# An mLSTM cell with a multiplicative FFN: where the rest products stand, what fills step 2, and how the denominator is computed

## The chip, the cores and the metric

The kernel runs on one core of one Trainium2 chip. The core has five instruction streams that run side by side and wait for one another through semaphores: PE (TensorE, matrix products; PEld is its weight loading), DVE (VectorE), ACT (ScalarE), POOL (GpSimd) and SP (SyncE, which issues most DMA transfers). The metric is the time on the device in microseconds (us), the median over runs of the same kernel. A profile is one execution, taken down instruction by instruction.

## The reference

The first part is an mLSTM cell with batch 4, 8 heads, 768 time steps and head dimension 40. For every head it carries a matrix state C, a vector n and a running maximum m:

```python
m_new = max(f + m, i);  f_stab = exp(f + m - m_new);  i_stab = exp(i - m_new)
C = f_stab * C + i_stab * outer(v, k);   n = f_stab * n + i_stab * k
denom = max(abs(n . q), 1.0)
y = sigmoid(o) * (C @ q) / denom
```

The outputs y of 8 heads side by side make rows of 320 numbers, 3072 of them (4 x 768). The second part is a feed-forward network on these rows x, with 1024 hidden columns:

```python
out = ((x @ w1) * (x @ w2)) @ w3 @ w_out
```

All arrays that the kernel reads and writes hold float32 numbers, except that the four weight matrices come as 64-bit words, which the kernel has to turn into float32 itself.

## The kernel before, in words

**The cell.** The recurrence is computed in chunks of 64 time steps. Two chunks (128 rows, one per partition) of one batch with all 8 heads are a unit; there are 24 units n, n = 4c + b for the pair of chunks c (0 to 5) and the batch b. The main loop runs over steps s = 0 to 31 (L820). `quarter_work(s)` (L338) treats two units in one step: the outputs of unit s - 1 and the scores of unit s.

For the outputs TensorE computes `ph` (weights `pw` times values `v`, L363) and `pi` (queries times the carried state, L366). Both lie in the bank pair `cell[1]` of the products' memory: `pi` in columns 0 to 164, `ph` in columns 164 to 328. For the scores it computes `ss` (keys times queries, L389) and `pc` (values times keys, the state's update, L394) in `cell[0]`. In the traces `ph` and `pi` from unit 2 on are called `cell<-v_all,pw` and `cell<-state,qT`, and `ss` and `pc` `cell<-qT,kT` and `cell<-vw,kbuf`.

VectorE follows with `outputs()` (L419): `h` is `pi` scaled by a gate (L423) with `ph` added in four pieces (L430). Each value tile has a 41st column that is filled with ones, so column 40 of `h` is n . q, the number whose absolute value goes into the denominator. The generator `steps()` hands out the denominator's passes one at a time, so that they can be put between others: the absolute value (L438, 8 numbers per row), max with 1 and times 2 (L440), the reciprocal (L441) together with e = (tanh(o/2) + 1) x that (L443, 320 numbers per row), and y = h x e (L445, 320 numbers). The gate o was turned into tanh(o/2) on ScalarE (L270). Between these passes stand `first_read` (L397, which multiplies the scores by the weights) and the two additions to the state (L404 or L406, and L414). The units' y is brought to the FFN's layout: for units 0 to 14 by transposes on TensorE (`px`, L485) and a copy on ScalarE (`xT`, L486), for the later ones by way of DRAM.

**The FFN.** `w3 @ w_out` is computed once, in 8 pieces `wp` (L263) into `w3o`, as the weights arrive: ScalarE and VectorE turn each weight tile into float32 (`scale`, `convert`; VectorE's lines L199 and L200, and L248 which transposes w3). The products x @ w1 and x @ w2 (`pa` and `pb`) need 320 rows of the weights: two full slices of 128 (`up`, L628) and a rest of 64. The rest of both matrices stands in one tile `wr`, and the products with it are of 64x64 tiles of TensorE's array, four of which can work beside each other. They are made by `up_rest` (L634; 16 products a block, then ScalarE's copy L638 and VectorE's product L639) in steps 2 to 15, and by `left` inside `up_by_seven` (L721; 32 products, then four additions on VectorE, by the helper's lines L686 and L684) from step 19 on. `up_by_seven` makes the full slices of the later token groups with seven products for eight. `ffn_out` makes the down-projection `po` and ScalarE copies it out as `o_sb` (L741), and sends it off (L743). From step 19 to step 24 the down-projection lies in `cell[1]`, columns 0 to 320 (L871).

**How a step is put together.** The list `n_up` gives one block of `up` in each of the steps 2 to 5 and two in each of the steps 6 to 15; `n_seven` gives one `up_by_seven` to each of the steps 19 to 30; `n_down` gives two down-projections to the steps 16 to 20 and one to 21 to 24. In a step TensorE first does the folding `wp`, the full slices and the down-projections; then `quarter_work` is called, which calls `rest()` (L883: `up_rest` of the step's blocks, or `left`), then `ph` and `pi`, then `ss` and `pc`. Step 2 is special: between its outputs and its scores it calls `between()` (L892), which makes the first transposes of y, converts weights, and does its own block of `up`.

**What sets the order.** `in_order` (L84) ties every matrix product to the one before it, so TensorE works in the order of the program's text. The other engines keep the program's order too, up to the places marked with `issue_after`, which let instructions be put behind a given one. A pool of four rotating banks (`mps`, L77) holds all products other than the cell's; a product that takes a bank has to wait until the reader of that bank's last content is done. Where `cell` is used, the wait is for that pair's last reader.

`warm(n, m, small)` (L97) makes products that nobody reads: n of 128x512 and `small` ones of 64x64 with 64 columns. `between()` calls `warm(1, small=38)` between the transposes of units 0 and 1. `rows_of_u(n)` (L293) is one VectorE transpose of 128x512 (L295) that prepares the weights of unit n.

Of the kernel before, what the change touches and what calls it, by code (L numbers as in the profile page):

```python
# [16 lines left out]
def kernel(  # L17
# [26 lines left out]
    nc = tc.nc  # L44
# [46 lines left out]
    def mm(out, lhsT, rhs, start=True, stop=True):  # L91
        in_order(nc.tensor.matmul(out, lhsT=lhsT, rhs=rhs, start=start, stop=stop))  # L92
# [1 line left out]
    def transpose(out, in_, n=P):  # L94
        in_order(nc.tensor.transpose(out, in_, ident[0:n, 0:n]))  # L95

    def warm(n, m=4, small=0):  # L97
        bank = mps([P, 4, P], "fill")
        for _ in range(n):
            mm(bank[:, 0:m], ident, ident.unsqueeze(1).to_broadcast([P, m, P]))  # L100
        for i in range(small):
            r = halves[i % 2]
            mm(bank[r, 0, 0:L], ident[r, 0:L], ident[r, 0:L])

    halves = [slice(0, L), slice(L, P)]
    heads = [slice(0, D), slice(DP, DP + D)]
# [231 lines left out]
    def quarter_work(s, rest, between, late):  # L338


        rest()

        def part(j, c0, n):
            return cell[j][:, :, c0:c0 + NP * n].rearrange("p x (n d) -> p x n d", d=n)

# [21 lines left out]
        den = None  # L367
        if 0 <= s - 1 < NU:
            den = outputs(s - 1, pi, ph)
            den()  # L370
            if between:
                for _ in range(3):
                    den()
                den = None
                between()
            if late:
                late()
# [41 lines left out]
    def outputs(n, pi, ph):  # L419
        c, b = divmod(n, B)  # L420
        hs = slice(b * H, (b + 1) * H)
        h = sb.tile([P, H, D1], FP, name="h", tag="h")
        nc.vector.tensor_tensor(out=h.rearrange("p (n two) d -> p two n d", two=2), in0=pi,  # L423
                                in1=gT[:, c, hs].rearrange("p (n two) -> p two n", two=2).unsqueeze(3)
                                .to_broadcast([P, 2, NP, D1]), op=OP.mult)
        if n < N_DIAG:
            nc.vector.tensor_tensor(out=h, in0=ph, in1=h, op=OP.add)
        for x, e in quarters if n >= N_DIAG else ():
            part = h[halves[x], 0:H // 2] if x == e else h[halves[x], H // 2:H]
            nc.vector.tensor_tensor(out=part, in0=ph[x][halves[e]], in1=part, op=OP.add)  # L430

        den = sb.tile([P, H, 1], FP, name="den", tag="den")

        def steps():
            V = nc.vector
            yield V.tensor_scalar(out=den.bitcast(U32), in0=h[:, :, D:D1].bitcast(U32), scalar1=0x7FFFFFFF, scalar2=None,  # L438
                            op0=OP.bitwise_and)
            yield V.tensor_scalar(out=den, in0=den, scalar1=1.0, scalar2=2.0, op0=OP.max, op1=OP.mult)  # L440
            yield V.reciprocal(out=den, in_=den)  # L441
            e = o_t.pop(n)
            nc.vector.scalar_tensor_tensor(out=e, in0=e, scalar=1.0, in1=den.to_broadcast([P, H, D]), op0=OP.add, op1=OP.mult)  # L443
            y_t[n] = sb.tile([P, DM + REM], FP, name="y", tag="y")
            yield nc.vector.tensor_tensor(out=y_t[n][:, 0:DM].rearrange("p (h d) -> p h d", d=D), in0=h[:, :, 0:D],  # L445
                                           in1=e, op=OP.mult)

        done = steps()
        return lambda: next(done)

# [80 lines left out]
        if i < NBQ:  # L531
            nc.gpsimd.memset(qbuf[i][:, :, D:DP], 0.0)
    for i in range(NBV):
        nc.gpsimd.memset(vbuf[i][:, :, D:D1], 1.0)
    for t in state:
        nc.gpsimd.memset(t[0], 0.0)
    nc.gpsimd.memset(gates[:, 5 * TC:2 * TB], 0.0)
# [282 lines left out]
    for s in range(len(n_up)):  # L820
# [71 lines left out]
        def between():  # L892
            twice(1)
            weighted(2)
            rows_of_u(3)
            for _ in range(3):
                scale_next()
            for n in range(2):
                x_trans(n)
                if n == 0:  # L900
                    warm(1, small=38)
            for _ in range(3):
                convert()
            turn(2)
            block = up(*now[0])
            weighted(3)
# [105 lines left out]
```

## Time and profile before

| what | value |
|---|---|
| time, median of 3 runs | 426.51 us (425.51 to 427.06) |
| span of the profiled execution (first to last instruction) | 425.8 us, .7 under the median; the profile gives no other time of its own |
| mean granted clock of TensorE | 0.996 |
| TensorE busy | 414.1 us, 97% |
| VectorE busy | 313.5 us, 74% |
| ScalarE, GpSimd busy | 150.1 and 154.3 us, 35% and 36% |
| L438, L440, L441 (denominator, 8 numbers): median of 24 | .17, .16, .19 us |
| L443, L445 (320 numbers): median of 24 | .76 and .82 us (.49 to 1.44) |
| DMA | 51.15 MB, 120 GB/s on the mean |

A line of a timeline holds the start in us, the duration, the engine, the line of the program, the operation, what it writes and reads, the shape, and how many such instructions the line sums up (x16). In brackets stand the idle time of the engine just ahead and what ended it: `[0.58 <-DVE ab L639]` is .58 us of waiting for VectorE's instruction of line 639 that writes `ab`. "issue" is a wait for which the profile shows no other instruction. The products of one group overlap, so the next group's start says more than a duration added to a start.

### The profile page before, as it was taken

How to read it: one execution, taken by the hardware profiler on the slowest of the kernel's cores; microseconds unless marked ns; L12 is line 12 of the kernel's file. 1: busy time of each engine (PE TensorE's matmuls, PEld its weight loads, DVE VectorE, ACT ScalarE, POOL GpSimd, SP SyncE). 2: the span in 40 equal slices, each digit the busy share in tenths (PEclk: the TensorE clock that was granted, in tenths of full speed). 3: DMA queues.
4: the chain of work that ended last, by engine and by line, in shares of the span. 5: the costliest groups of instructions: out<-in, count | busy, mean ns of one | idle time of the engine just before them, and what ended most of it. 6: DMA issues, size and time to landing. Idle time of an engine off the chain costs nothing.

```text
span 425.8 us, 13079 instructions
## 1 busy us (share of the span) xinstructions
PE 414.1 (97%) x5353; PEld 335.3 (79%) x5353; DVE 313.5 (74%) x635; ACT 150.1 (35%) x404; POOL 154.3 (36%) x211
## 2 busy tenths in 40 slices
PE   7989989999999999999999999999999999999996
PEld 4768878888688788787777778788778879888896
DVE  6676986888949779778736966596868699575971
ACT  4766865567723623630433313032311110210000
POOL 4421342233303303303307751546453587542100
PEclk9989999999999999999999999999999999999999
DMA  8999998598977776985425675756421120000001
GB/s 186 204 173 245 214 144 140 134 193 180 215 183 154 166 182 135 181 164 105 89 80 130 153 141 121 142 133 117 87 44 36 35 39 2 31 2 31 2 32 62
DMA packets 135211, 51.15 MB, mean 120 GB/s; under 512 B 109360, under 2 KB 126960, under 8 KB 135152
## 3 DMA queue, kind: packets, MB, share of 16 engines
q1 hardware_dynamic: 131552, 46.29, 53.9%
q10 hardware_dynamic: 3600, 4.03, 2.7%
q8 instruction: 42, 0.69, 0.7%
q14 instruction: 17, 0.14, 0.1%
HBM read 44.50 MB, written 5.80 MB: 118 GB/s over the span
## 4 chain that ended last, share of the span: by engine, by line
PE 53%; issue 20%; DVE 7%; POOL 7%; SPq 7%; DMA 5%; ACT 1%; POOLq 0%; DVEq 0%
PE cell L92 17%; PE pa L92 12%; PE o L92 8%; PE pb L92 8%; PE p L92 3%; POOL pw L308 3%; SPq L184 3%; DVE w3T L666 2%; PE pt L95 1%; POOL vw L330 1%; SPq L148 1%; DMA raw<-in_moe_w_dram 1%; PE fill L92 1%; POOL raw L659 1%; POOL state L335 1%
## 5 line engine op out<-in xcount | busy, mean ns | idle before, releaser
L335 POOL TENSOR_TENSOR state<-state,decay 128x164 f32<-128x164 f32 x40 | 20.0, 500 | 154.8 <-DVE state L404 129.0
L92 PE MATMUL pa<-xT,w 128*128 128x256 f32 x240 | 60.4, 382 | 0.0
L92 PEld LDWEIGHTS pa<-xT,w 128*128 128x128 f32 x240 | 44.4, 190 | 6.8 <-DVE h L430 0.4
L303 ACT ACTIVATE pw<-pw,aT 128x64 f32<-128x64 f32 x184 | 46.4, 339 | 3.2 <-ACT o_sb L741 1.9
L92 PE MATMUL pb<-xT,w 128*128 128x256 f32 x192 | 45.4, 379 | 0.0
L729 POOL TENSOR_TENSOR ab<-ab,a_sb 128x512 f32<-128x512 f32 x22 | 29.4, 1356 | 32.2 <-DVE ab L684 32.2
L92 PEld LDWEIGHTS pb<-xT,w 128*128 128x128 f32 x192 | 36.4, 190 | 5.0
L711 POOL TENSOR_TENSOR wo<-wo 128x512 f32<-128x512 f32 x22 | 27.4, 1268 | 29.8 <-DVE wo L686 29.8
L92 PE MATMUL pa<-xT,wr 64*64 64x256 f32 x384 | 37.0, 386 | 0.5 <-DVE wr L200 0.5
L92 PE MATMUL wp<-wo,w3T 128*128 128x320 f32 x128 | 35.9, 433 | 1.1 <-DVE ab L639 0.6
L308 POOL TENSOR_SCALAR_AFFINE_SELECT pw<-pw 64x512 f32<-64x512 f32 x48 | 35.8, 746 | 3.0 <-ACT pw L303 1.2
L92 PE MATMUL pb<-xT,wr 64*64 64x256 f32 x384 | 36.4, 380 | 0.0
L92 PE MATMUL cell<-w3o,ab 128*128 128x320 f32 x128 | 35.4, 432 | 0.0
L638 ACT ACTIVATE a_sb<-pa 128x512 f32<-128x512 f32 x24 | 14.3, 598 | 59.0 <-PE pb L92 59.0
L639 DVE TENSOR_TENSOR ab<-pb,a_sb 128x512 f32<-128x512 f32 x24 | 16.4, 688 | 23.2 <-ACT a_sb L638 22.8
L92 PEld LDWEIGHTS wp<-wo,w3T 128*128 128x128 f32 x128 | 23.8, 190 | 10.5 <-DVE ab L639 0.8
L92 PEld LDWEIGHTS cell<-w3o,ab 128*128 128x128 f32 x128 | 24.3, 190 | 9.5
L92 PEld LDWEIGHTS pa<-xT,wr 64*64 64x64 f32 x384 | 18.9, 132 | 15.4 <-issue 8.8
L686 DVE SCALAR_TENSOR_TENSOR a_sb<-pa,wo 128x512 f32<-128x512 f32 x12 | 8.3, 689 | 29.8 <-PE pa L92 29.8
L430 DVE TENSOR_TENSOR h<-cell,h 64x164 f32<-64x164 f32 x88 | 28.6, 326 | 1.6
L92 PE MATMUL po<-w3o,ab 128*128 128x320 f32 x96 | 26.4, 433 | 0.0
L92 PEld LDWEIGHTS po<-w3o,ab 128*128 128x128 f32 x96 | 18.1, 190 | 7.3
(180 smaller groups left out, 846.4 us busy)
## 6 DMA issues: line engine op xcount, KB each, us to landing
raw<-in_moe_w_dram SPq DMA_DIRECT2D x64, 128.0 KB, 3.4
kbuf<-in_k_dram SPq DMA_DIRECT2D x24, 160.0 KB, 4.5
v_all<-in_v_dram SPq DMA_DIRECT2D x24, 160.0 KB, 4.9
o_in<-in_o_gate_dram SPq DMA_DIRECT2D x24, 160.0 KB, 4.8
pw<-U_d SPq DMA_DIRECT2D x28, 128.0 KB, 3.5
raw<-in_moe_w_dram SPq DMA_DIRECT2D x5, 512.0 KB, 6.7
raw<-in_moe_w_out_dram SPq DMA_DIRECT2D x8, 320.0 KB, 4.1
gates<-in_k_dram SPq DMA_DIRECT2D x28, 80.0 KB, 2.5
```

What stands on the lines that cost most here:

```text
L92: in_order(nc.tensor.matmul(out, lhsT=lhsT, rhs=rhs, start=start, stop=stop))
L184: nc.sync.dma_start(out=dst, in_=src)
L303: nc.scalar.activation(out=pw[:, h, :], in_=src[:, h, :], func=AF.Exp, bias=aT[:, c, b * H + h:b * H + h + 1])
L308: nc.gpsimd.affine_select(out=pw[r], in_=pw[r], compare_op=OP.is_ge, fill=0.0, base=0, pattern=[[0, H], [1, L]], channel_multiplier=-1)
L335: nc.gpsimd.tensor_tensor(out=new, in0=old, op=OP.mult, in1=decay[:, b * NP:(b + 1) * NP, 2 * c + x:2 * c + x + 1] .to_broadcast([P, NP, D1]))
L430: nc.vector.tensor_tensor(out=part, in0=ph[x][halves[e]], in1=part, op=OP.add)
L638: nc.scalar.mul(out=a_sb, in_=pa, mul=UP ** -2)
L639: nc.vector.tensor_tensor(out=ab_t[gr][j][:, fs[0]:fs[-1] + 1, t0:t0 + a_sb.shape[-1]], in0=pb, in1=a_sb, op=OP.mult)
L666: nc.vector.tensor_tensor(out=dst, in0=p, in1=q, op=OP.subtract)
L686: nc.vector.scalar_tensor_tensor(out=out, in0=p, scalar=UP ** -2, in1=q, op0=OP.mult, op1=OP.add)
L711: aside_by.tensor_tensor(out=kept[j][:, 1:4:2], in0=kept[j][:, 1:3], in1=kept[j][:, 3:4].to_broadcast([128, 2, TH]), op=OP.add)
L729: aside_by.tensor_tensor(out=t[:, f:FO:FH, :], in0=t[:, f:FO:FH, :], in1=a, op=OP.mult)
```

## The change

There are four edits.

1. `rest()` is no longer called first in `quarter_work`, but after the products `ph` and `pi` and VectorE's `h`. TensorE's order in a step becomes: full slices, down-projection, `ph`, `pi`, rest products, `ss`, `pc`. On VectorE `h` (L423, L430) stands ahead of L639, or of the four additions of `left`; the denominator's passes follow these.
2. In `between()`, `warm(1, small=38)` becomes `warm(2)`: the 38 small products go and one more of 128x512 is made.
3. In `between()`, `rows_of_u(3)` stands behind the three `convert()`.
4. The denominator takes four passes for five. The values' 41st column holds 2 in place of 1, so column 40 of `h` is 2r with r = n . q. The passes are: the reciprocal 1/(2r); its absolute value (8 numbers each); v = min(that, .5) x h (320 numbers); y = (tanh(o/2) + 1) x v (320 numbers). Since .5 / max(|r|, 1) = min(1/(2|r|), .5), y is the same. In the program's order the pass that makes v stands where the reciprocal's step ended, ahead of the second state addition (L414).

```diff
-    def warm(n, m=4, small=0):
+    def warm(n, m=4):
         bank = mps([P, 4, P], "fill")
         for _ in range(n):
             mm(bank[:, 0:m], ident, ident.unsqueeze(1).to_broadcast([P, m, P]))
-        for i in range(small):
-            r = halves[i % 2]
-            mm(bank[r, 0, 0:L], ident[r, 0:L], ident[r, 0:L])
...
     def quarter_work(s, rest, between, late):
-        rest()
...
             den = outputs(s - 1, pi, ph)
+        rest()
+        if den:
             den()
...
-            yield V.tensor_scalar(out=den.bitcast(U32), in0=h[:, :, D:D1].bitcast(U32), scalar1=0x7FFFFFFF, scalar2=None,
-                            op0=OP.bitwise_and)
-            yield V.tensor_scalar(out=den, in0=den, scalar1=1.0, scalar2=2.0, op0=OP.max, op1=OP.mult)
-            yield V.reciprocal(out=den, in_=den)
-            e = o_t.pop(n)
-            nc.vector.scalar_tensor_tensor(out=e, in0=e, scalar=1.0, in1=den.to_broadcast([P, H, D]), op0=OP.add, op1=OP.mult)
+            yield V.reciprocal(out=den, in_=h[:, :, D:D1])
+            yield V.scalar_tensor_tensor(out=den, in0=den, scalar=-1.0, in1=den, op0=OP.mult, op1=OP.max)
+            v = h[:, :, 0:D]
+            yield V.scalar_tensor_tensor(out=v, in0=den.to_broadcast([P, H, D]), scalar=0.5, in1=v, op0=OP.min, op1=OP.mult)
             y_t[n] = sb.tile([P, DM + REM], FP, name="y", tag="y")
-            yield nc.vector.tensor_tensor(out=y_t[n][:, 0:DM].rearrange("p (h d) -> p h d", d=D), in0=h[:, :, 0:D],
-                                           in1=e, op=OP.mult)
+            yield V.scalar_tensor_tensor(out=y_t[n][:, 0:DM].rearrange("p (h d) -> p h d", d=D), in0=o_t.pop(n), scalar=1.0, in1=v,
+                                         op0=OP.add, op1=OP.mult)
...
-        nc.gpsimd.memset(vbuf[i][:, :, D:D1], 1.0)
+        nc.gpsimd.memset(vbuf[i][:, :, D:D1], 2.0)
...
         def between():
             twice(1)
             weighted(2)
-            rows_of_u(3)
             for _ in range(3):
                 scale_next()
             for n in range(2):
                 x_trans(n)
                 if n == 0:
-                    warm(1, small=38)
+                    warm(2)
             for _ in range(3):
                 convert()
+            rows_of_u(3)
             turn(2)
```

Two consequences follow. The line numbers of the changed kernel are 3 to 5 smaller from `warm` on. And since the state's columns are made from the same value tiles, the state's 41st column is doubled as well.

## The prediction

> **What bounds the kernel now.** I read the page first: its busy line, and the clock row beside it (PEclk is 9, full, in all slices but the third, an 8).
>
> ```profile
> PE 414.1 (97%) x5353; PEld 335.3 (79%) x5353; DVE 313.5 (74%) x635; ACT 150.1 (35%) x404; POOL 154.3 (36%) x211
> ```
>
> TensorE is busy for 414.1 of the span's 425.8 us at a full clock, so 11.7 us in all can be saved by waiting less; anything that makes TensorE wait anew lengthens the kernel one for one. An engine off TensorE's path can lose time for nothing. The chain of waits says the same (PE 53%, DVE 7%, ACT 1%), so from here I read only the timelines of TensorE and, around the moved instructions, those of its partners.
>
> The outputs' products `ph` lie in the bank pair `cell[1]`, columns 164 to 328; from step 19 on the down-projection uses columns 0 to 320 of the same pair, and ScalarE has to copy it out (L741) before `ph` may write. TensorE's timeline of step 19, then ScalarE's for the same stretch:
>
> ```profile
> 256.62 0.70 PE L92 MATMUL cell<-w3o,ab 128*128 128x320 f32 x2
> 257.25 1.10 PE L92 MATMUL pa<-xT,wr 64*64 64x256 f32 x16
> 258.17 1.04 PE L92 MATMUL pb<-xT,wr 64*64 64x256 f32 x16
> 259.03 0.63 PE L92 MATMUL cell<-v_all,pw 64*64 64x41 f32 x32
> ```
>
> ```profile
> 257.36 0.43 ACT L741 COPY o_sb<-cell 128x320 f32<-128x320 f32 x1 [9.27 <-PE cell L92]
> 257.82 0.34 ACTq L743 DMA_DIRECT2D out_dram<-o_sb  x1
> 258.20 0.43 ACT L741 COPY o_sb<-cell 128x320 f32<-128x320 f32 x1 [0.41 <-ACT o_sb L741]
> ```
>
> Both copies start after the whole burst of down-projections and end at 258.63; the 32 rest products cover that, so `ph` at 259.03 waits for nothing.
>
> The second place is where VectorE converts w3 ahead of steps 8 and 9's adds; its timeline behind step 9's products, then TensorE's:
>
> ```profile
> 106.59 1.13 DVE L248 STREAM_TRANSPOSE w3T<-w 128x512 f32<-128x512 f32 x1
> 107.65 1.24 DVE L639 TENSOR_TENSOR ab<-pb,a_sb 128x512 f32<-128x512 f32 x2
> 108.81 0.48 DVE L423 TENSOR_TENSOR h<-cell,gT 128x328 f32<-128x328 f32 x1
> 109.33 1.34 DVE L430 TENSOR_TENSOR h<-cell,h 64x164 f32<-64x164 f32 x4
> ```
>
> ```profile
> 107.22 0.55 PE L95 MATMUL px<-ident,y 128*128 128x128 f32 x3
> 108.35 8.88 PE L92 MATMUL wp<-wo,w3T 128*128 128x320 f32 x32 [0.58 <-DVE ab L639]
> ```
>
> `wp` takes a bank that the first L639 frees: TensorE already waits 0.58 us for it here. The third is step 2, with the tiny products that go:
>
> ```profile
> 22.96 0.83 PE L95 MATMUL px<-ident,y 128*128 128x128 f32 x3 [1.19 <-DVE y L445]
> 23.59 4.90 PE L92 MATMUL fill<-ident 128*128 128x512 f32 x78
> 28.41 0.55 PE L95 MATMUL px<-ident,y 128*128 128x128 f32 x3
> ```
>
> **Part 1, rest() behind ph and pi, steps 19 to 24: +5.2 us.** Nothing now lies between the down-projection and `ph`, so each of these steps waits for the copies. From the rows: end of the last copy less the start of the next product, 258.62 - 257.25 = 1.37 and 277.07 - 275.70 = 1.37 with two copies, and .53 in each of the four steps with one (289.84 to 290.37, 303.97 to 304.50, 318.10 to 318.63, 332.23 to 332.77). Together 4.9, and .05 each for the release (px starts .05 after y's end at 22.91): 5.2. Bounds 4.9 to 5.6 (.12 each). The rest products take as long as before, behind the wait instead of in it. Queued behind the waiting `ph` on TensorE: pi, rest, ss, pc, the whole step; who waits for these in turn is part 2.
>
> **Part 2, the adds of the rest products come later on VectorE: +1.7.** VectorE now does h (.49 + 1.34) before the adds L686/L684. Counted from ph's start: h starts at +1.21 (in step 16, without rest products, `ph` starts at 218.20 and h at 219.41), ends at +3.09, the first add ends at +3.7, the others .6 apart, the fourth at +5.5. The next step's first `pa` takes the bank that the first add frees, and TensorE comes to it at +3.60 (260.85 - 259.03 for ph to pc, and 1.78 of rest products): +.15 with the release in each of steps 19 to 23, .75. In step 25 the product `p` takes such a bank. On the old times, step 24's `ph` would start at 332.23 + .58 = 332.8; TensorE comes to `p` after ph, pi (1.02) and the rest (1.78) at 335.7, the add ends at 332.8 + 3.7 = 336.5, and with the release it is +.95. Bounds .5 (only the last, and half of it) to 2.2 (.25 in the five). In steps 6, 7 and 10 to 15 the first add L639 ends at +3.7 to +3.8 and the next `pt` or `wp` wants it at +4.0: nothing, .27 to spare. Steps 16 to 18 have no rest.
>
> **Part 3, the same in steps 8 and 9: +2.05.** VectorE's conversions hold it to 107.72. Then h (.48 + 1.34, 1.85 with the starts) now goes ahead of L639, which is what `wp` waits for: 108.35 becomes 110.2, +1.85. One step earlier the conversions end at 92.94, .6 after pi: +.2. Bounds 1.2 (the conversions start earlier by the .63 us that VectorE is idle ahead of them at 100.28) to 2.6 (a bank of the second L639, .6 later, is wanted as well).
>
> **Part 4, the tiny products, and U's rows: -0.8.** 28.41 - 23.59 = 4.8 us of products go, one 128x512 (.59 at full clock) comes. But px of y(1) needs y(1), which ends at 25.62; the new passes bring it to about 25.0 and the idle time of 1.19 before 22.96 down by some .8. `pa` of step 2 (29.67) could start near 26.7, since the xT copies stand behind ScalarE's scalings to 25.8: 3 us. Those 3 us meet the weights. ScalarE's timeline of steps 3 and 4:
>
> ```profile
> 42.48 0.69 ACT L191 ACTIVATE raw<-raw 128x512 f32<-128x512 f32 x1 [1.20 <-DMA raw<-in_moe_w_dram]
> ...
> 44.48 0.69 ACT L191 ACTIVATE raw<-raw 128x512 f32<-128x512 f32 x1 [0.74 <-DMA raw<-in_moe_w_dram]
> ```
>
> These tiles land when the DMA queue brings them (97% busy from 30 to 61 us), not when TensorE is early. `pb` of step 4 needs the first through VectorE (45.16 before, not ahead of 44.5), wr the second (47.27; TensorE waits .51 there, and that gap goes, since ph and pi now stand ahead of it). But L639 of step 4 stands behind h and ends near 51.2, so `pa` of step 5 starts where it did, 51.3. In step 5 the same reckoning gives `pa` of step 6 at 59.0 against 60.59, if TensorE's 1.49 us without instructions (57.57 to 59.05, cause "issue") falls into a wait. I take half, .8. Bounds -3.3 (the 3 us stay, and half of U's row, .70, which no longer stands ahead of three conversions) and +1.0 (nothing gained, and half clock, which the row below shows, for 2 us more while TensorE idles ahead of px). That every row counts, 8.0, is rival 3. rows_of_u(3) after the conversions delays weights(3) on ScalarE and masks(3) on POOL by 3.9 us (25.54 to 29.46) at the most; their first reader is L397 of step 3 at 45.08, and ph of step 4 at 48.24 the first on TensorE.
>
> **Part 5, order of tile shapes: +0.5.** From ph's start to pi's is .49 behind 128x128 products (218.20 to 218.69) and .44 behind 64x64 ones (259.03 to 259.47); .05 in the 19 steps with rest products ahead of ph is 1.0, and half of it where the step waits anyway. Bounds 0 to 1.5 (the change back to 128x128, now behind pc, costs too).
>
> **Part 6, four passes for five: 0.** .17 + .16 (L438, L440) go, one of 8 elements comes, two of 320 stay: .16 per step less on VectorE (74% busy). Its cover is TensorE's products: a pass of 320 now stands before the state add L414, which may end .3 to .7 later; what reads it has .25 or more in hand. If that is gone, .3 in each of 5 steps.
>
> **The clock, a rule against a row.** The windows (start:end, length, busy time of TensorE, its weight loads, VectorE, ScalarE and POOL, then the granted clock, DMA share and GB/s):
>
> ```profile
> 23.30:26.60 3.30, 3.30 (x26) 1.75 (x27) 2.98 (x9) 2.89 (x6) 0.30 (x2) 0.52 0.93 140
> 57.50:60.90 3.40, 1.92 (x30) 1.77 (x26) 3.29 (x11) 0.97 (x3) 0.00 (x0) 1.00 0.59 127
> ```
>
> In the first the granted clock is .52, behind the idle 1.19; in the second it is 1.00, though the idle 1.49 lies in it. By the first row each new wait of over 1.2 us could cost 3.3 x (1 - .52) = 1.6, by the second none. I take none: the second idle time is the longer one and stands, as the new waits do, between stretches of full work; the other end is rival 2. The Trainium skill ("TensorE: Matmul & The Clock Gate", "Why this matters for your kernels") says that TensorE should have no idle gap over about 3 us, since one idle window brings it back to half clock. By that rule alone the new waits (up to 2.4 us) cost no clock and the sum stays, but the same rule speaks against the change where it takes out products that fill a wait; the first row disagrees with it, the second agrees.
>
> **Sum.** 5.2 + 1.7 + 2.05 - .8 + .5 + 0 = 8.65 on the profiled 425.8, 434.45; the median of the runs (426.51) stands .7 above that span: 435.2.
>
> **Rivals.**
> 1. The early gain is carried (the 3.3 of part 4 in place of .8): 432.7. For: TensorE has 4.2 us less to do there. Against: the DMA landings above. 20 in 100.
> 2. The clock falls behind the new waits. For: half clock for 3.3 us behind an idle of 1.19. Places: behind step 9 (2.4 us idle) and steps 19 and 20 (1.4), 1.6 each: up to +4.8, 440.0. Against: full clock round the 1.49. 12 in 100.
> 3. The other side, not slower: TensorE starts step 2's blocks early and all of the head's idle is carried to the end: 4.8 + 1.19 + .51 + 1.49 = 8.0 in place of .8, sum +1.4, 427.9 or, if the adds cost the lower bounds too, 426. It decides (no slower than +.5%) from 7.3 carried. 5 in 100.
> 4. The change does not expose the copies: ScalarE copies each down-projection as it ends, and `ph` writes columns that are free. Without part 1: 430.0. Against: ScalarE's 9.27 us of waiting end .1 after the burst of all 16 products, not after its first half; and 164 to 328 lie within 0 to 320 but for 8 columns. 6 in 100.
>
> **How the numbers follow.** The forecast has 57 in 100. Its own bounds, added in squares about the sum (part 1 .4, 2 .8, 3 .7, 4 1.2, 5 .6), are some 1.8 either way; the range goes past rival 1 below, to 430.5, and to most of rival 2 above, 439.5 (two of its three places and the upper half of the bounds); what is left out, rivals 3 and 4 and the ends of the others, is 2 in 10. Half a percent, 2.1 us, is what a measurement here can tell from no change: same, .06, is rival 3 and the foot of 1; faster .03, the lower end of 3; slower .91.
>
> **What would show it.** Right: in steps 19 to 24 idle time of .5 to 1.5 before `cell<-v_all,pw`, put down to o_sb L741; before `wp` behind step 9 some 2.4 us put down to L639; `pa` of step 6 near 59; busy PE about 4 us less, idle about 13 more. Wrong: `ph` starting within .1 of the burst's end (part 1), `wp` unmoved (3), `pa` of step 6 at 57 or earlier (4), PEclk at half anywhere after 30 us.

## The result

The changed kernel takes 439.0 us (median of 4 runs, 436.51 to 440.52) where the kernel before takes 426.75: a ratio of 1.029 (95% interval 1.024 to 1.034), some 12.3 us more. The prediction was 435.2 us, with a range from 430.5 to 439.5. The direction is right, the range holds the time near its upper end, and the step is 12.3 us where 8.7 were worked out.

One thing has to be put right before the traces are compared. In every run whose span is known, the time is 1.8 to 2.1 us above the span. The execution that the prediction was read from (span 425.8) was therefore one of some 427.8 us, 1.2 above the median, and not .7 below it. The kernel before was profiled a second time (the run `b2_before`, 425.28 us, span 423.2). Its timeline has no wait of 1.49 us in step 5. The table takes both, since they differ in the first steps.

The profile's page of the changed kernel (busy us, share of the span, instructions; then the granted clock in 40 slices of the span):

```profile
PE 415.6 (95%) x5279; PEld 335.6 (77%) x5279; DVE 307.5 (70%) x611; ACT 149.5 (34%) x404; POOL 157.2 (36%) x211
PEclk9999999999899999999999999999999999999999
```

TensorE has 74 records of products fewer and is yet busy for 1.5 us more; its waits grew from 11.7 to 21.8 us. The 8 in the clock row is new: it lies at 109 to 120 us. The half clock of step 2 (24 to 27 us in the first profile of before) is not there.

Next, TensorE's and ScalarE's timelines of the changed kernel in step 19 (start, duration, engine, line, operation, tile written and read, shape, count; in brackets the idle time ahead and what ended it):

```profile
259.73 0.70 PE L92 MATMUL cell<-w3o,ab 128*128 128x320 f32 x2
261.79 0.68 PE L92 MATMUL cell<-v_all,pw 64*64 64x41 f32 x32 [1.35 <-ACT o_sb L736]
262.27 0.66 PE L92 MATMUL cell<-state,qT 40*64 40x41 f32 x32
262.74 1.07 PE L92 MATMUL pa<-xT,wr 64*64 64x256 f32 x16
263.63 1.04 PE L92 MATMUL pb<-xT,wr 64*64 64x256 f32 x16
...
265.72 0.70 PE L92 MATMUL pa<-xT,w 128*128 128x256 f32 x2 [0.27 <-DVE a_sb L681]
```

```profile
260.47 0.43 ACT L736 COPY o_sb<-cell 128x320 f32<-128x320 f32 x1 [9.40 <-PE cell L92]
260.93 0.34 ACTq L738 DMA_DIRECT2D out_dram<-o_sb  x1
261.31 0.43 ACT L736 COPY o_sb<-cell 128x320 f32<-128x320 f32 x1 [0.41 <-ACT o_sb L736]
```

The copies still start at the end of the burst, but the rest products now stand behind `ph`, and `ph` waits 1.35 us for the second copy. The next step's `pa` then waits .27 us for the first late add (L681). Over the steps 19 to 24 the waits ahead of `ph` are 1.35, 1.40, .56, .56, .52 and .56, those ahead of `pa` .27, .26, .26, .27 and .28. The profile names the copy for the first and the fifth wait of `ph` alone (for the others GpSimd's `wo`, or no cause), but in all six `ph` starts .05 to .10 us after the end of the step's last copy. Step 25 has the longest wait for an add:

```profile
346.77 0.70 PE L92 MATMUL p<-xT,w 128*128 128x256 f32 x2 [1.02 <-DVE a_sb L681]
```

Behind step 9, VectorE's timeline, TensorE's, and the windows around the wait (start:end, length, busy time of TensorE, weight loads, VectorE, ScalarE, POOL, then clock, DMA share, GB/s):

```profile
104.22 1.14 DVE L245 STREAM_TRANSPOSE w3T<-w 128x512 f32<-128x512 f32 x1
105.27 0.48 DVE L420 TENSOR_TENSOR h<-cell,gT 128x328 f32<-128x328 f32 x1
105.78 1.34 DVE L427 TENSOR_TENSOR h<-cell,h 64x164 f32<-64x164 f32 x4
107.16 1.29 DVE L634 TENSOR_TENSOR ab<-pb,a_sb 128x512 f32<-128x512 f32 x2
```

```profile
104.84 0.55 PE L95 MATMUL px<-ident,y 128*128 128x128 f32 x3
107.90 4.65 PE L92 MATMUL wp<-wo,w3T 128*128 128x320 f32 x10 [2.51 <-DVE ab L634]
```

```profile
105.00:107.50 2.50, 0.39 (x3) 0.15 (x2) 2.39 (x7) 2.50 (x10) 0.00 (x0) 1.00 0.83 246
107.50:111.00 3.50, 3.10 (x8) 2.06 (x9) 3.15 (x9) 1.85 (x5) 1.33 (x2) 0.70 0.71 192
111.00:114.50 3.50, 3.50 (x12) 2.36 (x11) 3.26 (x6) 2.63 (x5) 2.26 (x4) 0.81 0.91 194
```

h now goes ahead of L634, and `wp` waits 2.51 us in place of .58. In the 7 us after the wait the granted clock is .70 and .81: 3.5 x .30 + 3.5 x .19 = 1.7 us lost.

Last, step 2, with the tiny products gone:

```profile
21.13 0.44 PE L95 MATMUL px<-ident,y 128*128 128x128 f32 x2 [0.39 <-DVE y L440]
21.94 0.33 PE L95 MATMUL px<-ident,y 128*128 128x128 f32 x1 [0.38 <-POOL y L471]
22.11 1.88 PE L92 MATMUL fill<-ident 128*128 128x512 f32 x4
23.83 0.56 PE L95 MATMUL px<-ident,y 128*128 128x128 f32 x3
```

How far the changed kernel's trace lies behind that of the kernel before, by the end of `pc` in each step (drift within the stretch; the forecast's terms beside it):

| stretch | forecast | against the first profile (425.8) | against the second (423.2) |
|---|---|---|---|
| start to end of step 9 | -.6 (part 4, and .2 of part 3) | -2.37 | +.50 |
| step 10 | +1.85 (part 3) | +3.62 | +3.72 |
| steps 11 to 18 | +.35 (of part 5) | +1.69 | +1.48 |
| step 19 to the end | +7.05 (parts 1, 2, .15 of 5) | +8.64 | +8.47 |
| sum | 8.65 | 11.6 | 14.2 |

### The profile page after: what moved, and what is told of

The parts are those of the page before. It is cut to its first block, busy times and chain, and to the rows that moved or that the text cites. A ratio compares the mean times of both kernels' runs of the same rounds, so it can differ in the third digit from the quotient of the medians.

```text
span 437.4 us, 12911 instructions
## 1 busy us (share of the span) xinstructions
PE 415.6 (95%) x5279; PEld 335.6 (77%) x5279; DVE 307.5 (70%) x611; ACT 149.5 (34%) x404; POOL 157.2 (36%) x211
## 4 chain that ended last, share of the span: by engine, by line
PE 64%; DVE 13%; SPq 9%; DMA 5%; issue 5%; POOL 2%; ACT 1%; DVEq 0%; ACTq 0%; POOLq 0%
PE cell L92 15%; PE pa L92 15%; PE pb L92 10%; PE wp L92 8%; PE o L92 8%; PE po L92 4%; SPq L136 4%; PE p L92 3%; SPq L181 2%; DVE h L427 2%; DVE w3T L661 2%; DMA raw<-in_moe_w_dram 2%; DMA wo<-in_moe_w_dram 1%; SPq L150 1%; DVE a_sb L681 1%
## 5 line engine op out<-in xcount | busy, mean ns | idle before, releaser
L332 POOL TENSOR_TENSOR state<-state,decay 128x164 f32<-128x164 f32 x40 | 22.6, 564 | 161.2 <-DVE state L401 101.5
L420 DVE TENSOR_TENSOR h<-cell,gT 128x328 f32<-128x328 f32 x24 | 11.9, 495 | 71.3 <-PE cell L92 71.2
L92 PE MATMUL wp<-wo,w3T 128*128 128x320 f32 x128 | 37.4, 449 | 2.5 <-DVE ab L634 2.5
L92 PEld LDWEIGHTS wp<-wo,w3T 128*128 128x128 f32 x128 | 24.7, 197 | 12.6 <-DVE ab L634 2.8
L92 PEld LDWEIGHTS pa<-xT,wr 64*64 64x64 f32 x384 | 20.1, 133 | 7.4 <-issue 2.3
L92 PEld LDWEIGHTS pb<-xT,wr 64*64 64x64 f32 x384 | 21.5, 133 | 2.1
```

The source lines that it names most:

```text
L332: nc.gpsimd.tensor_tensor(out=new, in0=old, op=OP.mult, in1=decay[:, b * NP:(b + 1) * NP, 2 * c + x:2 * c + x + 1] .to_broadcast([P, NP, D1]))
```

## The experiments

All the kernels compute the whole of the reference; some make products more that nobody reads. The ratios are to the kernel before, timed on the same chip beside them (its medians there were 426.97, 426.26 and 425.85 us in the three sets of runs).

### Which part loses the time: the rest products first again from step 19

```diff
     def quarter_work(s, rest, between, late):
+        if s >= 19:
+            rest()
...
-        rest()
+        if not (s >= 19):
+            rest()
```

> The changed kernel, but from step 19 on the rest products stand ahead of ph and pi again. The changed kernel took 439.0 us; in its trace the steps 19 to 24 wait 4.95 us for o_sb's copies and, up to the product p of step 25, 2.36 us for the late adds, and the two traces drift apart there by 8.8 us in all (from 2.94 to 11.74). Theory: both waits come from the place of the rest products, and the 1.5 us beyond the marked waits are overlap of neighbouring products lost at each wait. Then all 8.8 go: 430.2 us (429 to 431.5), no wait over .1 us ahead of ph or pa in these steps. Rival: the 1.5 us, or the waits for the adds, belong to the denominator's new passes on VectorE, which stay here: then only the copies' 4.95 go, 434 us, and waits of some .27 us ahead of pa stay.

Measured: 431.34 us (430.06 to 434.07), ratio 1.011 (1.008 to 1.014). No wait over .1 us stands ahead of `ph` or `pa` in these steps; the same place as above, in this kernel:

```profile
260.43 1.09 PE L92 MATMUL pa<-xT,wr 64*64 64x256 f32 x16
261.34 1.04 PE L92 MATMUL pb<-xT,wr 64*64 64x256 f32 x16
262.20 0.62 PE L92 MATMUL cell<-v_all,pw 64*64 64x41 f32 x32
```

From the end of step 18 to the end the trace is .1 us from the first profile of before, where the changed kernel lost 8.6. The medians differ by 7.7. So the waits for the copies and for the adds come from the move, and the 1.2 us that the steps lose beyond the marked waits (8.5 to 8.6 against 4.95 + 2.36) go with them; the four passes, which stayed, take no part. In the trace of before, neighbouring groups overlap a little (the down-projections end at 257.32, the next products start at 257.25); behind a wait they don't. Twelve waits at .1 each is an account of the 1.2, not a measurement.

### Steps 8 and 9 alone put back

The edit is as above with the condition `s in (8, 9)`.

> The changed kernel, but in steps 8 and 9 the rest products stand ahead of ph and pi again. In the changed kernel's trace wp behind step 9 waits 2.51 us (.58 before), and in the 7 us after that the granted clock is .70 and .81; between the ends of steps 9 and 10 the traces drift by 3.62 us. Theory: 1.93 of these are the wait for L634 behind h, and 1.7 the lower clock that the wait brings. Then wp waits about .6, the clock is 1.00 there, and the time falls by 3.6: 435.4 us (434 to 436.5). Rival: the lower clock comes from something other than this wait (it comes and goes by itself): 437.1 us, and a window with a clock under .9 in some place.

Measured: 437.32 us (435.27 to 438.86), ratio 1.021 (1.014 to 1.028). The time can't tell the two apart. The timeline and the windows can:

```profile
107.19 8.88 PE L92 MATMUL wp<-wo,w3T 128*128 128x320 f32 x32 [0.68 <-DVE ab L637]
116.86 1.35 PE L92 MATMUL pa<-xT,w 128*128 128x256 f32 x5 [0.80 <-ACT xT L484]
```

```profile
107.50:111.00 3.50, 3.50 (x14) 2.47 (x13) 3.39 (x11) 2.11 (x4) 0.29 (x1) 1.00 0.82 218
111.00:114.50 3.50, 3.50 (x14) 2.47 (x13) 3.14 (x6) 1.26 (x2) 2.87 (x6) 1.00 0.61 203
```

The wait is .68, the clock full, and the drift within step 10 falls from 3.62 to 1.17. It doesn't fall to nothing, because a wait follows that nobody had forecast: TensorE now comes early to `pa` and waits .80 us there for the copy xT. This is taken up below.

### The clock: the wait filled with products

```diff
-    def x_trans(n):
+    def x_trans(n, fill=0):
...
         px = mps([128, KF + 1, P], "px")
+        for _ in range(fill):
+            mm(px, ident, ident.unsqueeze(1).to_broadcast([P, KF + 1, P]))
...
         while s >= N_DVE and turned < min(s - 2, NY):
-            x_trans(turned)
+            x_trans(turned, 3 if s == N_DVE else 0)
```

A first run had 14 of these products.

> The changed kernel with 14 products of 128x384 that nobody reads, written into px's bank ahead of px behind step 9, about 2.2 us of work that lies where TensorE now waits 2.51 us for L634. The end of the wait is set by VectorE, so it should not move. Theory: the lower clock after the wait (.70 and .81 in the two windows of 3.5 us) is a matter of TensorE's idle time; with the fill the clock stays at 1.00 and the time falls by 1.7: 437.3 us (436.5 to 438). Rival: the clock falls whatever TensorE does there, or wp is slow for its weight loads beside the DMA: no change, 439.0 us. If the fill itself is late, the time rises.

Measured: 442.69 us (441.93 to 443.86), ratio 1.034 (1.027 to 1.040). The dose was wrong: a float32 product is two records in the trace, the 14 took 9.1 us and overran the wait. The clock stayed full. With 3 of them:

> The changed kernel with 3 products of 128x384 that nobody reads ahead of px behind step 9: by the run with 14 of them (28 records, 9.1 us) one takes .65 us, so 1.95 us of the wait of 2.51 are filled, where 14 overran it by 6.6. Theory: the clock stays at 1.00 in the windows behind, as it did with the 14, and the time falls by the 1.7 of the lower clock: 437.3 us where the changed kernel has 439.0 (436.5 to 438). Rival: the lower clock costs the kernel nothing because VectorE or the landings hold the next products anyway: 439.0.

Measured: 437.49 us (436.82 to 440.37), ratio 1.026 (1.023 to 1.029). TensorE's timeline and the windows behind the wait:

```profile
105.28 2.20 PE L92 MATMUL px<-ident 128*128 128x384 f32 x6
107.32 0.49 PE L95 MATMUL px<-ident,y 128*128 128x128 f32 x3
108.30 8.88 PE L92 MATMUL wp<-wo,w3T 128*128 128x320 f32 x32 [0.49 <-DVE ab L636]
```

```profile
108.00:111.50 3.50, 3.20 (x12) 2.33 (x13) 3.14 (x9) 2.21 (x5) 1.33 (x2) 1.00 0.76 205
111.50:115.00 3.50, 3.50 (x15) 2.47 (x14) 3.26 (x6) 2.78 (x6) 2.29 (x4) 1.00 0.99 182
```

`wp` starts where VectorE lets it, its 32 products take 8.88 us where they took 10.57, and the drift within step 10 is 1.89, the wait alone. All six runs had a mean clock of .999 or 1.000, three of the changed kernel's four .995 or .996. The median is 1.5 us lower, but the intervals of the two ratios overlap, so the price is better read from the profiles: 1.7 us. The lower clock is a matter of the idle time, and products that nobody reads prevented it here. It does not come in each execution: the changed kernel's run with a clock of 1.000 had a span of 434.6, and in the run `e7_move` below the same wait of 2.51 us has a full clock behind it.

The clock's records show the difference. In all fourteen profiles the granted clock is either full or half, and from one change to the next it always lasts a whole number of periods of 3.41 us (one at half clock in most places, two or three in `e3_down_first` and `e11_small_later`). The periods around the wait, in the changed kernel and then in `e7_move`, with their edges counted on from the profile's own changes:

```profile
105.51:108.93 3.42, 1.03 (x4) 0.79 (x5) 3.31 (x9) 3.42 (x10) 0.00 (x0) 1.00 0.92 240
108.93:112.34 3.41, 3.41 (x8) 2.10 (x7) 3.06 (x8) 1.59 (x3) 2.28 (x5) 0.50 0.64 195
112.34:115.75 3.41, 3.41 (x14) 2.41 (x13) 3.17 (x5) 1.97 (x4) 1.31 (x2) 1.00 1.17 178
```

```profile
103.66:107.07 3.41, 2.79 (x98) 2.06 (x87) 3.20 (x6) 2.43 (x8) 0.00 (x0) 1.00 0.72 196
107.07:110.49 3.42, 1.53 (x6) 1.14 (x7) 3.35 (x11) 3.34 (x8) 0.00 (x0) 1.00 0.83 229
```

In the changed kernel TensorE is idle for 2.39 us within one period, and one period of half clock follows (3.41 x .5 = 1.7 us lost). In `e7_move` an edge divides the wait into .6 and 1.9 us, and the clock stays full. In all fourteen profiles, once the clock was full, each period with 2.1 us or more of idle time was followed by half clock. With .9 to 1.95 us some were and some were not, and these runs don't show what decides there.

### Another cover for the copies: the down-projections first

```diff
             if s <= NU:
+                ffn_out([downs.pop(0) for _ in range(n_down[s])], [cell[1][:, i, 0:DM] for i in range(2)])
                 seven[0]()
             seven[1]()
-        if seven and s <= NU:
-            ffn_out([downs.pop(0) for _ in range(n_down[s])], [cell[1][:, i, 0:DM] for i in range(2)])
-        else:
+        if not (seven and s <= NU):
```

> The changed kernel, but in steps 19 to 24 the down-projections are made first in the step, ahead of the products of up_by_seven, so that these cover o_sb's copies; the rest products stay behind ph and pi. Theory: the waits for the copies (4.95 us) and for the first add ahead of pa (1.34 us in five steps) go, and with them their lost overlap of some 1.1; the wait ahead of p in step 25 (1.02) stays: 431.6 us (430.5 to 433). Rival: another wait takes their place, because the copies of p15 (L699), which share the bank pair with ph, now come last: some .5 us ahead of ph in each of six steps, 434.6 us.

Measured: 439.61 us (438.86 to 442.94), ratio 1.028 (1.020 to 1.035): nothing won. TensorE's timeline in steps 19 and 23:

```profile
247.07 5.17 PE L92 MATMUL cell<-w3o,ab 128*128 128x320 f32 x9 [2.87 <-DVE h L427]
...
318.69 2.96 PE L92 MATMUL cell<-w3o,ab 128*128 128x320 f32 x10 [1.38 <-POOL ab L724]
```

In steps 20 to 22 the theory holds: there is no wait ahead of `ph` or `pa`, and these steps drift by .10, .11 and .10 us where the changed kernel drifted by 1.93, 1.09 and .96. But in step 19 the down-projection comes to `cell[1]` before h of the step ahead has read it (2.87 us, and a clock of .50 and .68 in the 7 us behind), and in step 23 before GpSimd has made its input (1.38 us). The wait ahead of `p` in step 25 grew from 1.02 to 1.52 us. Neither theory had these: both looked at who waits for the moved work, and not at what the moved work itself waits for.

### The move alone

```diff
     def quarter_work(s, rest, between, late):
-        rest()
...
             den = outputs(s - 1, pi, ph)
+        rest()
+        if den:
             den()
```

> The kernel before with edit 1 alone: the rest products behind ph and pi, the tiny products and the five passes kept. Theory: all the lost time comes from the move: 8.8 us in steps 19 to 25, 1.9 of waiting and 1.7 of lower clock behind step 9, less the .5 of the wait for wr in step 4: some 12 us over the kernel before, 438.9 us (437.5 to 440.5). Rival: the move costs only what the marked waits hold (7.3 and 1.9) and the rest came with the other edits: 436 us.

Measured: 437.73 us (436.97 to 439.64), ratio 1.026 (1.023 to 1.029): 11.5 us over the kernel before. This is the theory's time, and nearly the whole of the change's. In its profile `wp` waits 2.51 us too, but the clock is 1.00 in the two windows behind, and step 10 drifts by 1.94.

### Edits 2 to 4 without the move, and edit 2 alone

The first has `rest()` at the head of `quarter_work` in every step; the second is the kernel before with

```diff
-                    warm(1, small=38)
+                    warm(2)
```

> The changed kernel with the rest products ahead of ph and pi in every step: edits 2 to 4 without edit 1. In the changed kernel's trace the end of step 8 comes 1.9 us earlier than before, and the weights' landings in steps 3 and 4 only .5 to .7 earlier. Theory: this gain belongs to the tiny products (edit 2) and to the earlier y, not to the move, and nothing else of edits 2 to 4 costs time on TensorE: 1.5 to 2 us under the kernel before, 425.2 us where before is 427.0 (424.5 to 426). Rival: the landings take back the rest once TensorE waits for wr ahead of ph again (.51 us in step 4): no change, 427.0.

Measured: 429.32 us (428.5 to 431.01), ratio 1.006 (1.004 to 1.009).

> The kernel before with edit 2 alone: two products of 128x512 in place of one and 38 tiny ones in step 2. Theory: the early gain of the changed kernel is from here, but y of the second unit is still as late as before: TensorE idles ahead of the second px, 1.2 to 1.5 us of the gain at the end of step 8 stay: 425.6 us where before is 427.0. Rival: the gain is lost at the weights' landings: 427.0. If the clock falls at that idle time, it may be lost too.

Measured: 428.86 us (428.34 to 430.0), ratio 1.005 (1.002 to 1.008). Here theory and rival fell in both runs: the edits that take work away are 3.1 and 2.6 us slower than the kernel before, without the move. Their end of step 9 lies 2.9 and 3.0 us ahead of the first profile of before, and .0 and .1 from the second. The early gain belonged to that first profile. What then is lost can be read from step 10 of `e4_no_move`, TensorE's and ScalarE's timelines:

```profile
116.07 1.99 PE L92 MATMUL pa<-xT,w 128*128 128x256 f32 x8 [1.59 <-ACT xT L484]
```

```profile
109.70 0.68 ACT L188 ACTIVATE raw<-raw 128x512 f32<-128x512 f32 x1 [2.93 <-DMA raw<-in_moe_w_dram]
...
114.43 0.67 ACT L188 ACTIVATE raw<-raw 128x512 f32<-128x512 f32 x1 [1.24 <-DMA raw<-in_moe_w_dram]
115.00 0.66 ACT L192 ACTIVATE raw<-raw 128x512 uint32<-128x512 uint32 x1
115.56 0.46 ACT L484 COPY xT<-px 128x384 f32<-128x384 f32 x1
```

The copy that `pa` needs stands on ScalarE behind scalings of weight tiles that have not landed (in the run with edit 2 alone the wait is 2.06 us). And there are waits with no released cause ("issue") of 1.94 and .59 us in steps 12 and 15 (.96 and .57 in the run with edit 2 alone), the first followed by a clock of .54 for 3.7 us.

### The copy xT ahead of the scalings

Edits 2 to 4 without the move, and step 10's `px` and its copy put at the end of step 9, ahead of the weights and scalings:

```diff
-        if s + 1 < N_DVE:
+        if s + 1 <= N_DVE:
             while turned < min(s - 1, NY):
                 x_trans(turned)
                 turned += 1
-            if s not in (1, 2):
+            if s not in (1, 2) and s + 1 < N_DVE:
```

> Edits 2 to 4 without the move (as in the run e4_no_move, 429.3 us), but px of step 10 and its copy xT are put ahead of the weights and scalings on ScalarE's list, at the end of step 9. In e4_no_move TensorE waits 1.59 us ahead of pa of step 10 for this copy, which stands on ScalarE behind scalings that wait for raw tiles to land (109.7, 111.9, 114.4). Theory: the tiles' landings took back the early gain here, by way of ScalarE's order: the wait goes and 1 to 1.6 us stay to the end: 428.0 us (427.2 to 428.7). Rival: the landings hold the next conversions too (wp of steps 11 and 12): a wait of the same size turns up there, and the time stays at 429.3.

Measured: 427.29 us (424.5 to 430.25), ratio 1.003 (1.000 to 1.006), 2.0 us less than without, or 1.6 when each is set against the kernel before beside it; the intervals of the two ratios overlap. The copy stands at 105.93, and `pa` follows `wp` with no wait:

```profile
106.58 8.88 PE L92 MATMUL wp<-wo,w3T 128*128 128x320 f32 x32 [0.68 <-DVE ab L637]
115.29 1.89 PE L92 MATMUL pa<-xT,w 128*128 128x256 f32 x8
```

So this wait is gone, and by the medians it was a good part of what edits 2 to 4 lose without the move. The changed kernel itself doesn't have it: it comes to `pa` later, behind the wait ahead of `wp`. This is the one reason that was found why the parts don't add up: the move alone costs 11.5 us, the rest alone 3.1, and both together 12.3.

### Where the waits without a cause stand

Edits 2 to 4 without the move, and 38 small products behind `wp` of step 10, so that TensorE's later instructions have about the numbers of the kernel before:

```diff
         fold()
+        if s == N_DVE:
+            for _ in range(38):
+                mm(cell[0][:, 0, 448:512], ident, ident[:, 0:L])
```

> Edits 2 to 4 without the move (as in the run e4_no_move, 429.3 us), but 38 small products (128x64, two records each, nobody reads them) stand behind wp of step 10, where TensorE waits 1.59 us for the copy xT; they take some 2 us. TensorE's instructions from there on so have about the numbers that they have in the kernel before. Theory: the waits with no released cause (issue) in pc of step 12 and in step 15 (1.94 and .59 there; the first is at TensorE's product 2371 in all six traces without the tiny products that were looked at, and absent in the two with them) hang on the place in TensorE's instruction stream: they go, or move, and the time falls to 427.5 us (426.5 to 428.5). Rival: they hang on what else goes on at that time, such as the loads: they stay in pc of step 12, 429.5 us or a little more.

Measured: 434.7 us (433.94 to 441.64), ratio 1.020 (1.016 to 1.024). The dose was wrong again: the 76 records took 8.6 us and not 2. Its profile is of the longest execution (441.64 us), with a wait of 4.32 us at 47.5 us and half clock behind it; so only a place is read from it. The three lines are of this run, of the second profile of before, and of `e4_no_move`:

```profile
157.94 4.30 PE L92 MATMUL wp<-wo,w3T 128*128 128x320 f32 x15 [1.20 <-issue]
```

```profile
141.80 3.93 PE L92 MATMUL wp<-wo,w3T 128*128 128x320 f32 x14 [0.74 <-issue]
```

```profile
159.34 0.37 PE L92 MATMUL cell<-vw,kbuf 64*40 64x41 f32 x5 [1.94 <-issue]
```

Counted along TensorE's products, the wait of step 12 lies at product 2371 or 2372 in eight of the nine profiles without the tiny products (.56 to 1.94 us; `e8_fill` has none there). With them in step 2 it lies at 2244 (.54 to .74 in three profiles; none over .25 in the fourth, `e7_move`), and with 38 others put in later at 2245, in `wp` and no longer in `pc`. Its place hangs on the place in TensorE's stream of instructions.

The traces also show what the wait ends with. The page counts the packets of a queue of its own for instructions, in the changed kernel (packets, MB, share of 16 engines):

```profile
q8 instruction: 41, 0.67, 0.7%
```

These are 16 KB a packet, one every 10 us or so. From 25 us on, thirty waits of TensorE over .1 us have no released cause, those for the copies left out. In all thirty the next product starts 1.23 to 1.66 us after the end of such a packet:

| run, product | packet's end | TensorE ready | product starts | wait |
|---|---|---|---|---|
| `e4_no_move`, 2371 | 157.91 | 157.40 | 159.34 | 1.94 |
| `e6_warm`, 2371 | 157.07 | 157.47 | 158.43 | .96 |
| second profile of before, 2244 | 140.41 | 141.07 | 141.80 | .74 |
| `e7_move`, 2244 | 143.15 | 144.53 | 144.53 | none |
| `e8_fill`, 2371 | 160.25 | 164.06 | 164.06 | none |
| first profile of before, 977 (step 5) | 57.69 | 57.57 | 59.05 | 1.49 |
| second profile of before, 977 | 54.29 | 55.84 | 55.84 | none |

So the wait is as long as the packet is late. That TensorE waits for its own next instructions is what these times say; no run changed the packets, and what makes one late stays open.

### The denominator alone, and the kernel before once more

The kernel before with edit 4 only:

> The kernel before with edit 4 alone, the denominator in four passes. Theory: VectorE's passes lie beside TensorE's work, but for y of the first unit in step 2, where TensorE waits 1.19 us for it: at most .8 of that goes and the landings of the weights may take it back: 426.0 us where before is 426.3 (425.3 to 426.8). Rival: the pass of 320 numbers ahead of the second state addition delays the adds of the next step: .3 us in each of five steps, 427.8.

Measured: 426.56 us (423.6 to 431.1), ratio 1.000 (.997 to 1.004): no difference. The first wait for y in step 2 fell from 1.07 (second profile of before) to .39 and .38, and nothing of it is left at the end of step 9 (+.47).

> The kernel before, profiled once more. All its timed runs show a time 1.95 to 2.0 us over their span, so the profiled execution that the prediction was made on (span 425.8) is one of some 427.8 us, above the median. Theory: it held waits that most executions do not have, the 1.49 us of issue in step 5 above all: this profile has a span near 424.2 and no such wait over 1 us in that place. Rival: the wait is a fixed part of this program: it is there again, and the span differs elsewhere.

Measured: 425.28 us, span 423.2; no wait over .1 us in step 5, a full clock in step 2. The group with the tiny products (78 records) took 3.7 us there and not 4.9. The wait ahead of product 977 is gone because the packet of instructions came earlier (the last two rows above).

No kernel that was run is faster than the kernel before by more than the measurement can tell.

## Why the prediction was right, and where its sizes were off

**What bounds the kernel** held: TensorE is busy for 95% of the span, and every wait that was forecast for it lengthened the kernel at least one for one. But its busy time, forecast some 4 us lower, rose by 1.5: the half clock (1.7) and the overlap lost at each wait (1.2) were not in the sum.

**The range.** The mechanism (the copies, the late adds, the conversions) was right; that the time lies in the range is in part luck. The sum was 3.6 us short, twice the 1.8 that its own bounds gave. The range reached so far only because it was stretched for rival 2, which came true in one place.

**Part 1, +5.2:** the six waits are 4.95 us, 1.35 to 1.40 and .52 to .56 each, and each ends with a copy as forecast. Right. The cover was named from two lines, and `e1_first_late` gives it back.

**Part 2, +1.7:** 1.34 ahead of `pa` in five steps and 1.02 ahead of `p`, 2.36. The places and their order are right, the first size is not (.27 each for .15: the first add ends 3.87 us behind `ph`'s start and not 3.7). In step 14, where nothing was forecast, ScalarE's copy xT now ends at 181.36, behind a later copy of the rest products, and the weight loads for `pa` wait .52 for it; this costs .28 to .30 in all seven profiles with the move and nothing in the others. The step that was not in the sum at all is that TensorE loses more than the marked wait each time; parts 1 and 2 together were 6.9 and are 8.5.

**Part 3, +2.05:** 2.51 in place of .58 behind step 9, +1.93. Right, and `e2_first_8_9` takes it away.

**Part 4, -.8:** the forecast said that the weights' landings take the early 3 us back, and kept half of a wait of 1.49 us that the profile showed in step 5. The first half is shown: the tiles that landed for 42.48 and 44.48 land for 41.79 and 43.98, while TensorE's step 2 ended 4.2 us early (against the second profile, which has 41.44 and 43.61, they are late, though step 2 ends 2.2 us early). The second is the failed one: the 1.49 us was a matter of that execution, a packet of instructions that came late, as the second profile shows, and against that profile the changed kernel is .5 us late at the end of step 9. A gain from a wait that was seen once, with no released cause, should have been taken at zero. `pa` of step 6 starts at 58.59, near the 59 that was forecast, but the kernel before reaches it at 57.56 when the wait is not there. That the sum was set against a time .7 above the span, when it is 2.0, is of the same kind: an execution above the median was taken for one below it.

**Part 5, +.5:** nothing. `ph` takes .48 behind full-array products, as forecast, but whole steps of the same kind (11 and 13) last 15.29 us in both kernels.

**Part 6, 0:** right, by `e5_den`.

**The clock, 0:** the step that failed by most. The forecast took none of rival 2's loss, since a longer idle time than step 2's had left the clock full. The changed kernel's profile shows 1.7 us behind its longest wait, and the filled wait brings the clock back. This is also the one sign that the forecast had named as showing it wrong, half clock after 30 us. The row that it went by was no contrary case: its 1.49 us lie within one period of 3.41, where a lowered clock did not follow each time. Of rival 2's three places one came, and not in each execution. The Trainium skill ("TensorE: Matmul & The Clock Gate", "Why this matters for your kernels") puts the harmful gap at over some 3 us; the runs disagree, with half clock behind 2.51 us and, in `e4_no_move`, behind 1.94, and with a full clock behind 3.22 us in `e12_xT_first` (an edge divides it into 1.27 and 1.95). Another section of it ("Part 1: The HAM clock gate") says that the window is free-running, which fits what they show: the periods of 3.41 us, and a wait of 2.51 with a full clock behind it in `e7_move`, the same with a lowered one in the changed kernel.

**Rivals.** Rival 1 (the early gain is carried) is refuted by the second profile, rival 3 with it; rival 4 by the waits themselves. Rival 2 is right by a third of its size. What no case held is the shift of the waits in TensorE's own stream: step 12, where the wait of 1.24 us stands (.54 and .74 before), lasts 1.1 and .9 us longer, most of what steps 11 to 18 lose. The forecast saw only the one in step 5.

Left open is why the weight tiles of step 10 land 1.4 to 2.2 us later without the tiny products (the three scalings that wait for them start at 109.7, 111.9 and 114.4 in `e4_no_move`, at 108.3, 110.2 and 112.3 in the second profile of before, though TensorE ends step 9 at the same time in both). The twelve transfers are issued from 104.21 on in `e4_no_move` and from 102.44 on in the second profile of before, behind others on the same queue; the profiles don't show why those ahead took longer.

## What to carry to other kernels

Where one engine is busy throughout, ask of every group of its instructions what it covers: a copy, an add, a landing. Moving the group is free only if something else covers that, and the group put first has to be asked what it waits for itself. A gain at the start is worth nothing until the next transfer that sets the pace; look for the copy or conversion that queues behind it. And take two profiles of the kernel before: a wait without a released cause, and a clock that falls, can belong to one execution. Where a wait has no cause, look whether a packet of instructions has just landed.

## What the hardware showed that was not expected

The granted clock changed only at the edges of periods of 3.41 us. An idle time of TensorE of 2.48 to 2.51 us was followed by one period at half clock in the changed kernel and in `e1_first_late` and `e3_down_first` (2.26 to 2.39 us of it in one period), by none in `e7_move` (1.88). A wait of 2.87 us was followed by half clock, one of 3.22 us in `e12_xT_first` was not, and those of 1.07 to 1.19 us in step 2 were in two executions of four. A float32 product of 128x384 took .65 us and stands as two records. Taking 76 records out of TensorE's stream, with 2 put in, moved a wait of .5 to 1.9 us, for which the profile names no cause, from product 2244 to 2371. Thirty such waits ended 1.23 to 1.66 us after a packet of the instruction queue.
